# Cross attention and two expert layers on one core: the first layer's weights kept in single precision, a shorter first run of two batches, and the state rows prepared in two pieces

## The chip, the core and the metric

The kernel runs on one core of a Trainium2 chip. Five engines work side by side, each through its own instructions in order: TensorE (PE, matrix products), VectorE (DVE), ScalarE (ACT), GpSimd (POOL) and SyncE (SP), which here does nothing but start DMA transfers. An engine that needs another's result waits on a semaphore at the head of its queue, and all that stands behind the waiting instruction waits with it. The metric is device time in microseconds of one launch. The time before is the median of three runs; the profile is a fourth execution.

## The reference, cut to what matters

```python
# x: 8 batches, 8 heads, 512 tokens, 64 wide; state: 8, 8, 32, 64
a = softmax(x @ state^T / 8);   xread = a @ state          # "a" stage
a2 = softmax(state @ x^T / 8);  sread = a2 @ x             # "b" stage
z = concat(xread, sread)        # 8*512 + 8*32 = 4352 rows of 512
z = (sigmoid(z @ w_gate) * (z @ w_val)) @ w_out            # d_ff 1536
r = relu(z @ w_in); out = (r * r) @ w_out2                 # d_ff 2048
```

The expert weights arrive as float64, that is as two 32-bit words an element.

## The kernel before, in words

**Numbers.** Every product is made of three TensorE products of a value's high and low part: high by high, high by low, low by high (`mm3`, L183 to L185). A float64 weight tile of 128x512 is turned to these parts by a *conversion*: ACT extracts (L116, L118), DVE shapes and joins the bits (L119, L123, L127, L131) into a single-precision tile `c`, ACT casts its high part (L138), DVE subtracts for the low part (L139). `c` comes from a pool of two buffers.

**Layer 1 and its units.** The 1536 columns of layer 1 are 12 pieces f of 128; two pieces make one of six *chunks* (`ch`). The attention matrix `a` is not multiplied by the state first; the states are multiplied by the weights instead: for each chunk, `state_weights` multiplies four pairs of heads of four batches (m=0: batches 0 to 3, m=1: batches 4 to 7) by the chunk's converted weights; ACT copies the product from PSUM (`go`, L514, L518; with m=1 DVE makes the second copy), `store_g` writes it to memory (`gd`), and `load_g`, `split_gw` fetch it for one batch and one piece (`gi`, `gg`). A *unit* is one batch and one piece: `front_x` (six matmuls psg and a sigmoid on ACT, six matmuls psv, DVE's product, then the split into `gh` on ACT, L190, and `gl` on DVE, L191) and `back1` (twelve matmuls into `acc`). A unit is 24 matmuls of 512 columns. The converted weights, high and low, 512 KB a tile, go to memory once (`wd<-w`, 24 tiles). They are read again for m=1 (`wagain`, chunks 1 to 5) and for the state rows (`ws`).

**The order.** Units 0 to 23 are batches 0 to 3 with pieces 0 to 5 each (`HALF`), units 24 to 47 the same batches with pieces 6 to 11, units 48 to 95 batches 4 to 7 whole; 96 to 107 are the 256 state rows (`u_s` = 96), whose left operand is `sp`, the split of `xs_t`. All other work is handed out by `spread(steps, start, end)`, in units: chunk 2 from 1.2 to 3, the attention of batch 1 (`att_a[1]`) from 1 to 4, of batch 2 from 4 to 8, of batch 3 from 8 to 12, chunks 3 to 5 from 11.5 to 23.5, the m=1 chunks from 24.5 to 51.5, the state attention `att_b` from 45 + 5b. The last step of `att_b`, `b7`, copies a transposed piece to `xs_t` with four small copies, by turns on DVE (L467) and ACT (L465). A scheduler then fixes each engine's instructions in one order. Layer 2's weights are prepared in units 30 to 90 and layer 2 follows the state block.

Of the kernel before, what the change touches and what calls it, by code (L numbers as in the profile page):

```python
# [8 lines left out]
F32 = mybir.dt.float32  # L9
# [23 lines left out]
def kernel(  # L33
# [50 lines left out]
    xs_p = one.enter_context(tc.tile_pool(name="xsp", bufs=1, side="right"))  # L84
    aa_p = gen.enter_context(tc.tile_pool(name="aa", bufs=QB, side="right"))
    gi_p = gen.enter_context(tc.tile_pool(name="gi", bufs=2, side="right"))
    gg_p = gen.enter_context(tc.tile_pool(name="gg", bufs=2, side="right"))
    go_p = gen.enter_context(tc.tile_pool(name="go", bufs=3, side="right"))
    wr_p = gen2.enter_context(tc.tile_pool(name="wr", bufs=2, side="right"))
# [71 lines left out]
    def width(b):  # L161
# [6 lines left out]
    w_dram = {  # L168
        (ch, c): dram.tile([P, 2, 512], F32, name=f"wd{ch}_{c}")
        for ch in range(NCH) for c in range(NPAIR)  # L170
# [128 lines left out]
    def group_stages(b, g, both):  # L299
# [156 lines left out]
        def b7():  # L456
            w = v.pop("w")
            ps = at_p.tile([P, 2, 64], F32, tag="at", name="ps_so")
            nc.tensor.transpose(ps.rearrange("p a b -> p (a b)"), w, ident)
            for p in range(2):  # L460
                for i in range(2):
                    to = xs_t[D * p : D * (p + 1), 2 * g + i, b * NS : (b + 1) * NS]
                    src = ps[D * i : D * (i + 1), p, NS * i : NS * (i + 1)]
                    if i:
                        nc.scalar.copy(out=to, in_=src)  # L465
                    else:
                        nc.vector.tensor_copy(to, src)  # L467

# [31 lines left out]

    def conv_gv(ch, c, raw):
        gv[ch, c] = wr_p.tile([P, 2, 512], F32R, tag="w", name="w")
        convert(raw, gv[ch, c], False)

    def state_weights(ch, c, m):
        w = gv.pop((ch, c))
        if m == (ch < ONCE):
            nc.sync.dma_start(out=w_dram[ch, c], in_=w.bitcast(F32))
        ps = [at_p.tile([P, 512], F32, tag="at", name="ps_g") for j in range(2)]
        for j in range(2):  # L510
            sh, sl = (st_t[:, i, c, j, :] for i in range(2))
            mm3(ps[j], sh, sl, w[:, 0, :], w[:, 1, :], True, True)
        o = go_p.tile([P, 2, 512], F32, tag="go", name="go")
        nc.scalar.copy(out=o[:, 0, :], in_=ps[0])  # L514
        if m:
            nc.vector.tensor_copy(o[:, 1, :], ps[1])
        else:
            nc.scalar.copy(out=o[:, 1, :], in_=ps[1])  # L518
        g_out[ch, c, m] = o
# [11 lines left out]

    ONCE = 1

    def chunk_steps(ch, m, outs):
# [6 lines left out]
        def load(n):  # L541
            k, i = jobs[n]
            if ready:
                gv[ch, i] = raw_p.tile([P, 2, 512], F32R, tag="raw", name="wagain")
                nc.sync.dma_start(out=gv[ch, i].bitcast(F32), in_=w_dram[ch, i])
                return
            raws[n] = load_pair(ch, i) if k == "p" else load_raw(row_src(w_out1, i))

        def conv(n):
            k, i = jobs[n]  # L550
            if k == "p":
                conv_gv(ch, i, raws.pop(n))
            else:
                conv_out1(i, raws.pop(n))

        steps += [lambda: load(0), lambda: load(1)]
        for n in range(len(jobs) + 2):
            if n < len(jobs):
                if not ready:
                    steps.append(lambda n=n: conv(n))  # L560
                if not ready and n + 2 < len(jobs):
                    steps.append(lambda n=n: load(n + 2))
# [48 lines left out]

    def split_states():
        t = two["sp"].tile([P, 2, KD, NSTATE], F32R, name="sp")
        nc.scalar.copy(out=t[:, 0], in_=xs_t)
        nc.vector.tensor_sub(out=t[:, 1], in0=xs_t, in1=t[:, 0].bitcast(F32))
        s_parts["a"] = t

    def load_gv(ch, c):
        w = two["S"].tile([P, 2, 512], F32R, tag="w", name="ws")
        nc.sync.dma_start(out=w.bitcast(F32), in_=w_dram[ch, c])  # L620
        gv[ch, c] = w

    def front_s(b, f):
# [563 lines left out]

    HALF = NF1 // 2
    segments = [(b, 0, HALF) for b in range(QB)] + [(b, HALF, NF1) for b in range(QB)]
    segments += [(b, 0, NF1) for b in range(QB, B + 1)]  # L1190
# [38 lines left out]
    spread(chunk_steps(1, 0, outs[1]), 0, 1)  # L1229
    spread(chunk_steps(2, 0, outs[2]), 1.2, 3)  # L1230
    spread(att_a[1], 1, 4)
    spread(att_a[2], 4, 8)
    spread(att_a[3], 8, 12)
    for ch in range(3, NCH):
# [9 lines left out]
    for b in range(B):  # L1244
        start = 45 + 5 * b
        spread(att_b[b], start, start + 7)
# [5 lines left out]

    spread([close_gen], u_s - 0.6, u_s)
    spread([split_states], u_s - 0.55, u_s)
    spread([open_x_after_att], u_s - 0.5, u_s)
# [7 lines left out]
    for i, (b, f, lo, hi) in enumerate(units):  # L1263
# [7 lines left out]
        elif ff == 0:  # L1271
            for c in range(NPAIR):
                spread([lambda ch=ch, c=c: load_gv(ch, c)], max(i - 3, u_s - 0.4) + c / 50, i)
    for b in range(QB):
# [110 lines left out]
```

## Time and profile before

| what | value |
|---|---|
| runs | 1487.66, 1490.57, 1492.42 us; median 1490.57 |
| the profiled execution | 1494.57 us, span 1492.8 us |
| mean granted TensorE clock | 0.981 of full speed |
| units 0 to 23 start to end | 50.1 to 239.3 us |
| unit 5 / unit 9 / unit 24 start | 110.8 / 134.8 / 239.3 us |
| first matmul of the state block | 738.5 us |

The profiled execution lies 4.0 us above the median. A busy engine is one that runs an instruction; a wait is named by what ended it. The span's stages have different limits, so the stages are to be read one by one.

### The profile page before, as it was taken

To read this page: it belongs to the slowest core of one execution; us is meant where nothing else is said; L and a number is where in the kernel's file an instruction comes from. 1 tells how busy PE (TensorE), PEld (TensorE's weight loads), DVE (VectorE), ACT (ScalarE), POOL (GpSimd) and SP (SyncE) were. 2 spreads that over 40 slices of the span, in tenths; PEclk is the share of its full clock that TensorE was granted. 3 is DMA by queue.
4 is the path that set the end of the run, shared out by engine and by line. 5 is a ranking of instruction groups with operands and counts; after the bars stand their busy time and mean duration, and the time that the engine had idled before them with its cause. 6 is when DMAs were issued, how large, how long until landed. Compare 5 with 4: busy or idle time off the path is not lost.

```text
span 1492.8 us, 21831 instructions
## 1 busy us (share of the span) xinstructions
PE 1414.5 (95%) x7416; PEld 1204.0 (81%) x7416; DVE 1033.3 (69%) x1675; ACT 895.4 (60%) x1593; POOL 299.6 (20%) x264
## 2 busy tenths in 40 slices
PE   5769999999998889999899999899999999999998
PEld 3558878887787667888798888689999999988998
DVE  6886887568788998654534656665788479754665
ACT  6875877456668777654425855565566556564433
POOL 1112112233344454433103433200000000000000
PEclk9879999999999999999999999999999999999999
DMA  9995799699998885432586965765568555876675
GB/s 259 328 279 120 207 326 352 211 333 309 330 304 288 230 239 169 122 102 75 177 324 229 320 238 196 230 226 184 191 208 279 182 198 186 275 232 215 238 226 177
DMA packets 293375, 347.50 MB, mean 233 GB/s; under 512 B 108048, under 2 KB 204816, under 8 KB 293264
## 3 DMA queue, kind: packets, MB, share of 16 engines
q1 hardware_dynamic: 290992, 345.32, 72.1%
q8 instruction: 59, 0.97, 0.3%
q10 hardware_dynamic: 2272, 0.79, 0.2%
q14 instruction: 52, 0.43, 0.1%
HBM read 248.51 MB, written 97.52 MB: 232 GB/s over the span
## 4 chain that ended last, share of the span: by engine, by line
PE 70%; DMA 9%; DVE 9%; ACT 7%; issue 3%; POOL 1%; SPq 1%; DVEq 0%; ACTq 0%; POOLq 0%
PE o L185 7%; PE o L183 7%; PE o L184 7%; PE acc L183 4%; PE acc L184 4%; PE acc L185 4%; PE px L183 3%; PE px L184 3%; PE px L185 3%; PE psg L183 2%; PE psg L184 2%; PE psv L183 2%; PE psg L185 2%; PE psv L184 2%; PE psv L185 2%
## 5 line engine op out<-in xcount | busy, mean ns | idle before, releaser
L585 POOL TENSOR_TENSOR gg<-gi,gg 128x512 fp32r<-128x512 f32 x96 | 132.4, 1380 | 322.1 <-ACT gg L584 308.6
L183 PE MATMUL o<-wp,gh 128*128 128x256 f32 x672 | 188.8, 283 | 1.8 <-DMA wp<-wt 1.6
L184 PE MATMUL o<-wp,gh 128*128 128x256 f32 x672 | 188.7, 283 | 0.0
L185 PE MATMUL o<-wp,gl 128*128 128x256 f32 x672 | 185.4, 283 | 0.0
L184 PE MATMUL acc<-gl,o 128*128 128x512 f32 (+1 forms) x432 | 166.8, 387 | 6.4 <-DVE gl L191 6.2
L185 PE MATMUL acc<-gh,o 128*128 128x512 f32 (+1 forms) x432 | 164.9, 382 | 0.0
L183 PE MATMUL acc<-gh,o 128*128 128x512 f32 (+1 forms) x432 | 140.2, 381 | 2.1 <-ACT gh L190 2.1
L183 PEld LDWEIGHTS o<-wp,gh 128*128 128x128 f32 x672 | 128.3, 191 | 5.6 <-ACT g2s L964 1.4
L184 PEld LDWEIGHTS o<-wp,gh 128*128 128x128 f32 x672 | 128.5, 191 | 2.6
L185 PEld LDWEIGHTS o<-wp,gl 128*128 128x128 f32 x672 | 126.6, 191 | 1.2
L1090 DVE TENSOR_TENSOR y<-o,y 128x512 f32<-128x512 f32 x144 | 97.0, 685 | 35.1 <-PE o L185 34.3
L191 DVE TENSOR_TENSOR gl<-g,gh 128x512 fp32r<-128x512 f32 (+1 forms) x108 | 92.1, 853 | 28.2 <-ACT gh L190 27.6
L183 PE MATMUL px<-xh,wi 128*128 128x512 f32 x256 | 101.1, 396 | 6.0 <-DMA wi<-wi 5.0
L184 PEld LDWEIGHTS acc<-gl,o 128*128 128x128 f32 x432 | 82.5, 191 | 25.7 <-DVE gl L191 10.9
L184 PE MATMUL px<-xl,wi 128*128 128x512 f32 x256 | 100.9, 394 | 0.0
L185 PE MATMUL px<-xh,wi 128*128 128x512 f32 x256 | 100.1, 392 | 0.0
L606 DVE TENSOR_TENSOR g<-psv,sg 128x512 f32<-128x512 f32 x96 | 65.4, 682 | 46.6 <-PE psv L185 38.4
L183 PEld LDWEIGHTS acc<-gh,o 128*128 128x128 f32 x432 | 81.0, 189 | 18.2 <-ACT gh L190 2.7
L185 PEld LDWEIGHTS acc<-gh,o 128*128 128x128 f32 x432 | 82.5, 191 | 14.8
L190 ACT CAST gh<-g 128x512 fp32r<-128x512 f32 (+1 forms) x108 | 64.3, 596 | 47.0 <-DVE g L606 29.0
L599 ACT ACTIVATE sg<-psg 128x512 f32<-128x512 f32 x96 | 57.2, 596 | 55.4 <-PE psg L185 55.0
L183 PE MATMUL psg<-a,gg 128*128 128x512 f32 x192 | 77.5, 404 | 9.7 <-ACT sg L599 8.1
(215 smaller groups left out, 3793.1 us busy)
## 6 DMA issues: line engine op xcount, KB each, us to landing
wi<-wi SPq DMA_DIRECT2D x256, 256.0 KB, 3.9
gd<-go SPq DMA_DIRECT2D x192, 128.0 KB, 4.5
gi<-gd SPq DMA_DIRECT2D x96, 256.0 KB, 4.1
wp<-wt SPq DMA_DIRECT2D x96, 256.0 KB, 3.5
wp<-wo SPq DMA_DIRECT2D x72, 256.0 KB, 3.5
wi<-wa SPq DMA_DIRECT2D x32, 512.0 KB, 4.9
wo<-wo SPq DMA_DIRECT2D x32, 512.0 KB, 4.3
wd<-w SPq DMA_DIRECT2D x24, 512.0 KB, 4.9
```

The source lines that it names most:

```text
L183: nc.tensor.matmul(ps, lh, rh, start=start, stop=False, skip_group_check=more)
L184: nc.tensor.matmul(ps, lh, rl, start=False, stop=False, skip_group_check=more)
L185: nc.tensor.matmul(ps, ll, rh, start=False, stop=stop, skip_group_check=more)
L190: nc.scalar.copy(out=gh[:, :n], in_=g32[:, :n])
L191: nc.vector.tensor_sub(out=gl[:, :n], in0=g32[:, :n], in1=gh[:, :n].bitcast(F32))
L585: nc.gpsimd.tensor_sub(out=t[:, 1], in0=src, in1=t[:, 0].bitcast(F32))
L599: sig = nc.scalar.activation(out=sg, in_=ps, func=AF.Sigmoid)
L606: nc.vector.tensor_mul(out=g32, in0=ps, in1=sg)
L1090: nc.vector.tensor_add(out=y, in0=ps[to, j], in1=y)
```

## The change: what it does

The weights of layer 1 are kept in memory as the single-precision tile `c`: 256 KB instead of 512 KB. The store moves into the conversion and reads `c` itself. Who reads the tile again (`wagain`, `ws`) loads 256 KB and splits it once more, an ACT cast and a DVE subtraction (`split_again`). Units 0 to 3 are now batch 0 with pieces 0 to 3, units 4 to 7 batch 1 with pieces 0 to 3, 8 to 13 and 14 to 19 batches 2 and 3 with six pieces, 20 to 27 and 28 to 35 the remaining eight of batches 0 and 1, 36 to 47 the remaining six of 2 and 3. Chunk 2 is first needed by unit 12 instead of unit 4, the attention of batch 1 by unit 4 instead of 6, of batch 2 by 8 instead of 12, of batch 3 by 14 instead of 18. All four copies of `b7` are on ACT; the state attention starts two units sooner; `sp` is split for batches 0 to 6 first, batch 7 later.

```diff
-        (ch, c): dram.tile([P, 2, 512], F32, name=f"wd{ch}_{c}")
+        (ch, c): dram.tile([P, 512], F32, name=f"wd{ch}_{c}")
...
-                    if i:
-                        nc.scalar.copy(out=to, in_=src)
-                    else:
-                        nc.vector.tensor_copy(to, src)
+                    nc.scalar.copy(out=to, in_=src)
...
+    def conv_gv(ch, c, raw, m):
+        w = gv[ch, c] = wr_p.tile([P, 2, 512], F32R, tag="w", name="w")
+        cf = to_single(raw, False)
+        nc.scalar.copy(out=w[:, 0, :], in_=cf)
+        nc.vector.tensor_sub(out=w[:, 1, :], in0=cf, in1=w[:, 0, :].bitcast(F32))
+        if m == (ch < ONCE):
+            nc.sync.dma_start(out=w_dram[ch, c], in_=cf)
+
+    def split_again(w, sub):
+        nc.scalar.copy(out=w[:, 0, :], in_=w[:, 1, :].bitcast(F32))
+        sub(out=w[:, 1, :], in0=w[:, 1, :].bitcast(F32), in1=w[:, 0, :].bitcast(F32))
...
-        if m == (ch < ONCE):
-            nc.sync.dma_start(out=w_dram[ch, c], in_=w.bitcast(F32))
...
-                gv[ch, i] = raw_p.tile([P, 2, 512], F32R, tag="raw", name="wagain")
-                nc.sync.dma_start(out=gv[ch, i].bitcast(F32), in_=w_dram[ch, i])
+                w = gv[ch, i] = raw_p.tile([P, 2, 512], F32R, tag="raw", name="wagain")
+                nc.sync.dma_start(out=w[:, 1, :].bitcast(F32), in_=w_dram[ch, i])
...
-    HALF = NF1 // 2
-    segments = [(b, 0, HALF) for b in range(QB)] + [(b, HALF, NF1) for b in range(QB)]
+    FIRST = (4, 4, 6, 6)
+    segments = [(b, 0, FIRST[b]) for b in range(QB)] + [(b, FIRST[b], NF1) for b in range(QB)]
...
-    spread(chunk_steps(2, 0, outs[2]), 1.2, 3)
-    spread(att_a[1], 1, 4)
-    spread(att_a[2], 4, 8)
-    spread(att_a[3], 8, 12)
+    spread(chunk_steps(2, 0, outs[2]), 4, 7.5)
+    spread(att_a[1], 1, 2.6)
+    spread(att_a[2], 2.6, 5)
+    spread(att_a[3], 7, 10.5)
...
-        start = 45 + 5 * b
+        start = 43 + 5 * b
...
-    spread([close_gen], u_s - 0.6, u_s)
-    spread([split_states], u_s - 0.55, u_s)
+    spread([close_gen], u_s - 1.5, u_s)
+    spread([lambda: split_states(0, B - 1)], u_s - 1.4, u_s)
+    spread([lambda: split_states(B - 1, B)], u_s - 0.55, u_s)
...
-                spread([lambda ch=ch, c=c: load_gv(ch, c)], max(i - 3, u_s - 0.4) + c / 50, i)
+                at = max(i - 3, u_s - (0.6 if ch else 1.45))
+                spread([lambda ch=ch, c=c: load_gv(ch, c)], at + c / 50, i)
+                spread([lambda ch=ch, c=c: split_gv(ch, c)], min(at + 1, i - 0.4) + c / 50, i)
```

**TensorE around unit 4.** Before, the twelve matmuls of unit 3's `acc` are followed by batch 1's transposes (`ps_xt`) and scores (`ps_s`), and only then by unit 4, batch 0's piece 4, whose weights chunk 2 has made by then:

```order
L184 MATMUL acc_764<-gl,o_690 128x512
L185 MATMUL acc_764<-gh,o_690 128x512
L318 MATMUL ps_xt<-ident,xtok 128x128 x8
L183 MATMUL ps_s_1179<-xth,diag 128x512
L184 MATMUL ps_s_1179<-xtl,diag 128x512
L185 MATMUL ps_s_1179<-xth,diag 128x512
...
L183 MATMUL psg<-a,gg 128x512
```

In the changed kernel unit 4, now batch 1's piece 0, stands behind other scores, and chunk 2's first product `ps_g` comes only behind it:

```order
L185 MATMUL ps_s_955<-xth,diag 128x512
L183 MATMUL psg<-a,gg 128x512
L183 MATMUL psv<-a,gg 128x512
...
L185 MATMUL psv<-a,gg 128x512
L318 MATMUL ps_xt<-ident,xtok 128x128 x8
L183 MATMUL ps_s_1051<-xth,diag 128x512
...
L183 MATMUL ps_g<-w,st_t 128x512
```

Chunk 2 has moved from ahead of unit 4 to behind its start, and the second batch's attention from behind to ahead.

**ScalarE in an early conversion of layer 1's weights, ahead of unit 1.** Before, the step that fills the shared tile `c` (L118) waits for DVE alone:

```order
L116 ACTIVATE q<-raw 128x512 [waits DMAHW5_49,DMAHW2_49]
L369 CAST a<-a_417 128x512 [waits DVE_49]
L118 ACTIVATE c<-raw 128x512 [waits DVE_49]
L514 COPY go<-ps_g 128x512 [waits DMAHW6_49,DMAHW1_49,DMAHW7_49,DMAHW0_49,PE_49]
L518 COPY go<-ps_g 128x512 [waits PE_49]
L138 CAST w<-c 128x512 [waits DVE_49]
L116 ACTIVATE q<-raw 128x512 [waits DMAHW6_49,DMAHW5_49]
L118 ACTIVATE c<-raw 128x512 [waits DVE_49]
```

In the changed kernel it waits for the transfer (`DMAHW`) that reads the tile two conversions earlier; between that conversion's cast (L501) and the L118 stand eight other ACT instructions:

```order
L501 CAST w<-c 128x512 [waits DVE_49]
L337 COPY s_494<-ps_s_487 128x512 [waits DMAHW2_49,PE_49]
L116 ACTIVATE q<-raw 128x512 [waits DMAHW5_49,DMAHW2_49]
L369 CAST a<-a_417 128x512 [waits DVE_49]
L517 COPY go<-ps_g 128x512 [waits DMAHW6_49,DMAHW1_49,DMAHW7_49,DMAHW0_49,PE_49]
L521 COPY go<-ps_g 128x512 [waits PE_49]
L501 CAST w<-c 128x512 [waits DVE_49]
L116 ACTIVATE q<-raw 128x512 [waits DMAHW6_49,DMAHW5_49,Activation_49]
L351 ACTIVATE e_511<-e_511 128x512 [waits DVE_49]
L118 ACTIVATE c<-raw 128x512 [waits DMAHW3_49,Activation_49]
```

The wait for DVE has become a wait for a store.

**ScalarE ahead of the state block.** Before, the copies of the last `b7` alternate with DVE, and one cast makes `sp`:

```order
L465 COPY xs_t<-ps_so 64x32 [waits DVE_49]
L900 CAST xh<-xin 128x512
L900 CAST xh<-t 128x512
L465 COPY xs_t<-ps_so 64x32 [waits DVE_49]
L900 CAST xh<-t 128x512
L614 CAST sp<-xs_t 128x1024 [waits Activation_49]
```

In the changed kernel the cast of seven batches stands 16 rows ahead of that of the eighth, the repeated splits of the weights (`ws`) in between:

```order
L507 CAST ws<-ws 128x512 [waits DMAHW0_49]
L683 COPY y<-acc_7130 128x512 [waits PE_49]
L464 COPY xs_t<-ps_so 64x32 [waits PE_49]
L464 COPY xs_t<-ps_so 64x32 x3
L911 CAST xh<-xin 128x512
L507 CAST ws<-ws 128x512 [waits DMAHW1_49]
L507 CAST ws<-ws 128x512 [waits DMAHW2_49]
L623 CAST sp<-xs_t 128x4x32 [waits Activation_49]
```

The four copies now stand together, and the last cast is of 32 columns of each of four blocks.

## Rows read from the trace of the kernel before

**Rows 1.** The page: busy time of the engines; the chain; one kind of transfer.

```profile
PE 1414.5 (95%) x7416; PEld 1204.0 (81%) x7416; DVE 1033.3 (69%) x1675; ACT 895.4 (60%) x1593; POOL 299.6 (20%) x264
...
PE 70%; DMA 9%; DVE 9%; ACT 7%; issue 3%; POOL 1%; SPq 1%; DVEq 0%; ACTq 0%; POOLq 0%
...
wd<-w SPq DMA_DIRECT2D x24, 512.0 KB, 4.9
```

**Rows 2.** Windows by stage: us, busy of PE, PEld, DVE, ACT, POOL, clock, DMA, GB/s.

```profile
50.10:105.90 55.80, 41.66 (x168) 31.41 (x168) 47.89 (x91) 44.53 (x76) 8.01 (x8) 0.87 1.00 317
...
117.10:187.20 70.10, 70.10 (x311) 58.02 (x311) 52.43 (x87) 48.90 (x80) 15.22 (x15) 1.00 0.64 168
...
340.00:440.90 100.90, 98.11 (x432) 79.10 (x431) 81.61 (x131) 64.66 (x110) 35.62 (x33) 1.00 0.98 315
440.90:585.60 144.70, 127.80 (x560) 101.61 (x558) 130.09 (x210) 107.32 (x196) 70.95 (x57) 0.95 0.81 248
728.40:746.70 18.30, 12.81 (x59) 11.06 (x58) 10.46 (x19) 7.48 (x15) 0.00 (x0) 0.81 0.94 337
746.70:796.00 49.30, 49.30 (x405) 48.95 (x405) 15.67 (x34) 14.09 (x32) 0.00 (x0) 1.00 0.69 254
```

**Rows 3.** Groups of instructions in 50.1 to 105.9 us: busy, mean ns; idle before.

```profile
L116 ACT ACTIVATE q<-raw 128x512 uint16<-128x512 uint32 x12 | 9.3, 790 | 0.0
L131 DVE CUSTOM_DVE_ANT_0 c<-c,q 128x1024 uint16<-128x1024 uint16 x12 | 8.1, 682 | 0.1
L118 ACT ACTIVATE c<-raw 128x512 f32<-128x512 f32 x11 | 7.3, 662 | 0.9 <-DVE w L139 0.9
...
L127 DVE TENSOR_SCALAR q<-raw 128x512 uint16<-128x512 uint16 x12 | 5.4, 456 | 0.0
L139 DVE TENSOR_TENSOR w<-c,w 128x512 fp32r<-128x512 f32 x7 | 5.2, 740 | 0.8 <-ACT w L138 0.8
...
L119 DVE TENSOR_SCALAR c<-c 128x512 f32<-128x512 f32 x11 | 4.6, 417 | 1.4 <-ACT c L118 1.3
L123 DVE TENSOR_SCALAR c<-c 128x512 uint32<-128x512 uint32 x11 | 4.5, 418 | 0.1
L138 ACT CAST w<-c 128x512 fp32r<-128x512 f32 x7 | 4.4, 631 | 0.0
L325 DVE TENSOR_TENSOR xtl<-ps_xt,xth 128x512 fp32r<-128x512 f32 x6 | 4.0, 682 | 0.0
```

**Rows 4.** Timeline 84 to 106.5 us: start, length, instruction, idle before and its releaser.

```profile
94.67 1.06 PE L318 MATMUL ps_xt<-ident,xtok 128*128 128x128 f32 x8 [2.75 <-DMA xtok<-in_x_dram]
...
101.84 0.77 PE L183 MATMUL ps_s<-xth,diag 128*128 128x512 f32 x1 [6.11 <-DVE xtl L325]
...
105.93 0.79 PE L183 MATMUL psg<-a,gg 128*128 128x512 f32 x1 [1.19 <-ACT gg L584]
```

**Rows 5.** The stores of `wd` (512 KB) in 20 to 110 us: time to landing.

```profile
DMA to landing us min/median/max: 3.8/5.3/7.6
```

**Rows 6.** The stores of `sd` (256 KB) in the same stretch: time to landing.

```profile
DMA to landing us min/median/max: 2.2/3.8/6.9
```

**Rows 7.** The DVE copies of `b7`: count, min/median/max ns.

```profile
L467 DVE COPY xs_t<-ps_so x32: 144/183/185, 445.6 to 736.2; 64x32 f32<-64x32 f32 x32
```

**Rows 8.** The waits of TensorE in 440.9 to 585.6 us: total, times, longest.

```profile
PE psg L183 <- ACT sg L599: 7.0, 3, 2.9
PE acc L184 <- DVE gl L191: 5.2, 5, 2.2
```

**Rows 9.** One more subtraction of two SBUF tiles (layer 2's weights): min/median/max ns.

```profile
L748 DVE TENSOR_TENSOR wa<-c,wa x32: 649/684/1789, 289.4 to 569.1; 128x512 fp32r<-128x512 f32 x32
```

**Rows 10.** Timeline at the state block's start, 733 to 752 us.

```profile
738.50 0.58 PE L183 MATMUL psg<-sp,ws 128*128 128x256 f32 x1 [4.12 <-ACT sp L614]
739.40 1.22 DVE L615 TENSOR_TENSOR sp<-xs_t,sp 128x1024 fp32r<-128x1024 f32 x1
```

**Rows 11.** The loads of `ws` (512 KB) for the state block: time to landing.

```profile
DMA to landing us min/median/max: 3.2/6.6/9.4
```

More of the change, by code (lines that the diff above doesn't have):

```diff
@@ L85 @@
     aa_p = gen.enter_context(tc.tile_pool(name="aa", bufs=QB, side="right"))
+    go_p = gen.enter_context(tc.tile_pool(name="go", bufs=3, side="right"))
     gi_p = gen.enter_context(tc.tile_pool(name="gi", bufs=2, side="right"))
     gg_p = gen.enter_context(tc.tile_pool(name="gg", bufs=2, side="right"))
-    go_p = gen.enter_context(tc.tile_pool(name="go", bufs=3, side="right"))
     wr_p = gen2.enter_context(tc.tile_pool(name="wr", bufs=2, side="right"))
@@ L499 @@
     g_out = {}
-    def conv_gv(ch, c, raw):
-        gv[ch, c] = wr_p.tile([P, 2, 512], F32R, tag="w", name="w")
-        convert(raw, gv[ch, c], False)
+    def conv_gv(ch, c, raw, m):
[8 more added lines that the diff above has]
+        sub(out=w[:, 1, :], in0=w[:, 1, :].bitcast(F32), in1=w[:, 0, :].bitcast(F32))
     def state_weights(ch, c, m):
         w = gv.pop((ch, c))
-        if m == (ch < ONCE):
-            nc.sync.dma_start(out=w_dram[ch, c], in_=w.bitcast(F32))
         ps = [at_p.tile([P, 512], F32, tag="at", name="ps_g") for j in range(2)]
@@ L532 @@
     ONCE = 1
+    SUB2 = nc.vector.tensor_sub
     def chunk_steps(ch, m, outs):
@@ L551, in conv @@
             if k == "p":
-                conv_gv(ch, i, raws.pop(n))
+                conv_gv(ch, i, raws.pop(n), m)
             else:
@@ L558, in chunk_steps @@
             if n < len(jobs):
-                if not ready:
+                if ready:
+                    steps.append(lambda n=n: split_again(gv[ch, jobs[n][1]], SUB2))
+                else:
                     steps.append(lambda n=n: conv(n))
@@ L610, with split_states, split_gv @@
     s_parts = {}
[L612 to L616, printed above, removed]
+    def split_states(lo, hi):
+        if not s_parts:
+            s_parts["a"] = two["sp"].tile([P, 2, KD, NSTATE], F32R, name="sp")
+        cols = slice(lo * NS, hi * NS)
+        h, l = (s_parts["a"][:, i, :, cols] for i in range(2))
+        nc.scalar.copy(out=h, in_=xs_t[:, :, cols])
+        nc.vector.tensor_sub(out=l, in0=xs_t[:, :, cols], in1=h.bitcast(F32))
     def load_gv(ch, c):
         w = two["S"].tile([P, 2, 512], F32R, tag="w", name="ws")
-        nc.sync.dma_start(out=w.bitcast(F32), in_=w_dram[ch, c])
+        nc.sync.dma_start(out=w[:, 1, :].bitcast(F32), in_=w_dram[ch, c])
         gv[ch, c] = w
+    def split_gv(ch, c):
+        split_again(gv[ch, c], nc.vector.tensor_sub)
     def front_s(b, f):
```

## The prediction, made before the changed kernel ran

> **What bounds the kernel now.** The page says 95% for TensorE [rows 1], but the chain of work that ended last gives TensorE only 70%, and DMA, DVE and ACT 25% together [rows 1]: there are stages in which others set the end. The windows by stage show where. In units 0 to 3, 50.1 to 105.9 us, PE is busy 41.66 of 55.8 us, at a granted clock of 0.87, while DVE works 47.89 us (86%), ACT 44.53 (80%), and the DMA engines are busy all the time [rows 2]. From 117.1 to 187.2 us PE has no idle time. In 340 to 440.9 it lacks 2.8 us, in 440.9 to 585.6 16.9 us, with DVE at 130.09 of 144.7 (90%, the highest of any long stretch) [rows 2]. The last gap is the start of the state block, 728.4 to 746.7, where PE idles 5.5 us and the clock is 0.81 [rows 2]. So there are three places to win something, and the change touches each. The timeline of the first shows what PE waits for when unit 4 comes: an input tile from memory, DVE's `xtl`, then ACT's `gg` [rows 4]. These are small pieces of work behind much other work on busy engines and queues, and not one slow instruction.
>
> **Term 1: the first 24 units.** A conversion costs DVE 0.417 + 0.418 + 0.682 + 0.456 + 0.740 = 2.71 us and ACT 0.790 + 0.662 + 0.631 = 2.08 us [rows 3]. Chunk 2 has six. I counted the instructions ahead of unit 5's first psg in both programs. DVE has six conversions less, two subtractions of them excepted (12 x 0.417, 6 x 0.682, 6 x 0.456, 4 x 0.69: 14.6), and a few steps of a softmax less (1.8, at lengths like those of the other rows); it has two `xtl` and two copies of y more (4 x 0.68 = 2.7) [rows 3]. That is about 14 us less; ACT has some 12 us less. DVE was busy 86% of the stretch [rows 2], so unit 5 should start 14/0.88 = 16 us sooner: near 95 us instead of 110.8. The DMA gives the same: a chunk loads 3.1 MB, writes 2.1 MB of products, 1.05 MB of stores; 6 MB at 317 GB/s [rows 2] are 19 us of a full DMA.
>
> But the work isn't gone. By the same count DVE has, ahead of unit 9, as much to do as before (+1.6 us), and so has PE. Between the first psg of units 5 and 9 of the changed program stand 24.6 us of matmuls at full rate and 31 us of DVE work. If PE sets the pace unit 9 starts at 95 + 24.6 = 119.6; if DVE does, at its highest long share, 90% (440.9 to 585.6 us) [rows 2], at 95 + 34 = 129. Before, it started at 134.8. From unit 9 to 24 there are 101.3 us of matmuls where 104.5 us passed, with 87 us of DVE work. The stretch that is nearest is 50.1 to 105.9, where DVE set the pace, so I take a value near the DVE end: -8 us, bounds 0 and -18.
>
> **Term 2: units 29 to 80.** The repeated splits are 20 on ACT (0.63 each, like L138 [rows 3], 12.6 us) and 20 on DVE (0.68 each, like L748's median [rows 9], 13.7 us), in units 29 to 51.5, some 140 us. In 340 to 440.9 DVE is 19 us free and ACT 36 [rows 2], so most of it is covered by PE's work; without that cover it would cost up to 14 us. The 20 re-loads of 512 KB become 256 KB, in a stretch with the DMA at 0.98 [rows 2]: 5.2 MB less, 16 us of a full DMA. `b7` loses 32 DVE copies of 0.183 us [rows 7], 5.9 us, and the alternation with ACT; ACT gains as much. In 440.9 to 585.6 PE waits 7.0 us for ACT's sigmoid and 5.2 us for DVE's `gl` [rows 8]; the first may grow, the second shrink, and the state attention starting two units earlier moves work from the fullest stretch towards a freer one. I take -3 us, bounds -10 (most of the 12.2 us of waits gone) and +6.
>
> The Trainium skill speaks against this part: "SBUF — State Buffer", section "Who interferes with whom", has a DVE instruction with two SBUF inputs and a GpSimd instruction that reads SBUF exclude each other for their whole length. Here the longest subtraction of two SBUF tiles took 1.789 us against a median of 0.684 [rows 9], as that rule would have it, though no run here isolates it. By it the 20 subtractions could cost up to 20 x 1.1 = 22 us more of DVE. It is the third rival below.
>
> **Term 3: the state block.** Before, the last `ps_so` is followed by copies by turns, a cast and a subtraction of 1024 columns (1.04 us on ACT, 1.22 on DVE), and psg starts at 738.50 after 4.12 us of waiting; its second product waits for the subtraction [rows 10]. Now the cast of one batch's columns is left for the end (near 0.27 us), but seven or eight casts of `ws` at 0.63 and the four copies stand on ACT near it. Adding the ACT and DVE steps behind unit 95's psv up to the second product I get 11.3 us for 12.3: -1 us, bounds -3 and +3. In the state block itself PE is busy all 49.3 us, DVE 15.67, ACT 14.09 [rows 2]: 16 splits of 0.68 and 0.63 are covered. The loads halve (median landing 6.6 us [rows 11]), the split adds 1.3 us: 0, bounds 0 and +4.
>
> **Term 4: the tile that the store holds.** L118 now waits until the store of `c`, two conversions back, has landed. The 256 KB stores of `sd` took 3.8 us in the middle and 6.9 at most [rows 6], the 512 KB ones 5.3 and 7.6 [rows 5]. The eight ACT instructions between, at 0.6 to 0.8 us [rows 3], are 5.8 us in the place that the order rows show. Counted over all conversions with the work that stands between: at 5.5 us from the join to landing ACT would wait 10.6 us in sum over seven of them, at 8.0 us 41 us. At the middle the ACT waits lie in its free time (11 us in 50.1 to 105.9, 21 in 117.1 to 187.2 [rows 2]). I take 0, bounds 0 and +20.
>
> **Sum.** -8 - 3 - 1 + 0 = -12 us on the profiled execution's 1494.57 us: 1482.6. That execution lies 4.0 above the median of the runs, so against the median 1478.5 us.
>
> **Rivals.** (A) *Slower: the store holds ScalarE.* Its place is L118 in chunks 1 to 5, units 0 to 23. It decides when the stores land beyond about 6.5 us after the join; for it speak the DMA share of 1.00 and the maxima of 6.9 and 7.6 us; against it the medians. With 41 us of ACT waits, half passed on to PE through the sigmoids and casts queued behind, it is +20, less the gain of 12: +8, 1498.5 us. (B) *The gain is given back*: chunk 2 now meets the attention of batches 2 and 3 in units 4 to 11. In 117.1 to 187.2 DVE was 52.43 of 70.1 us busy; 14 us more makes 95%, above every stretch seen. Then term 1 falls to -1 and the sum to about -4: 1486.5. (C) *The second splits fill DVE*: 13.7 us and the longer subtractions, of which 19 us are free; term 2 becomes +6 and the sum -3: 1487.5. (D) *PE sets the pace all along*: -18 - 7 - 1 = -26: 1464.5.
>
> **Chances.** My forecast 0.56, D 0.12, B 0.12, C 0.07, A 0.13. What this kernel's runs can tell from no change is about 0.3%, 4.5 us. B and C lie at -3 to -4, partly over it: same 0.15; A holds cases from 0 to +20: slower 0.11; faster 0.74. The range leaves out the outer half of A and the lower part of D: 1464 to 1494.
>
> **What would show it.** In the changed profile, the start of unit 5 near 95 us (110.8), of unit 9 at 120 to 130 (134.8), of unit 24 near 231 (239.3) show term 1. If unit 9 is early and unit 24 is not, it is B. If L118's idle time has `wd` DMA as its releaser with over 15 us in sum, it is A. If the idle time of PE in 290 to 440 us grows and the subtractions of `wagain` average over 1 us, it is C. `b7` shows in the waits of 440.9 to 585.6 us (16.9 us of idle PE), the state block in the first psg (738.5) against the end of unit 95. The prediction fails if the early stretch is bound by latency of single loads and not by the work on DVE: then unit 5 moves by a few us only.

## The result, and the profile after

The changed kernel takes 1504.67 us (median of four runs, 1502.28 to 1507.23) against 1491.49 us before: a ratio of 1.0093, 95% interval 1.0064 to 1.0122. It is slower by 13 us where 12 us less was forecast, and lies outside the range.

The page of the changed kernel has TensorE as busy as before by share, and less of it in the chain than the 70% of [rows 1]:

```profile
PE 1423.6 (95%) x7416; PEld 1198.8 (80%) x7416; DVE 1057.7 (70%) x1688; ACT 925.7 (62%) x1672; POOL 301.1 (20%) x264
...
PE 62%; DMA 12%; DVE 11%; ACT 7%; issue 5%; SPq 2%; POOL 1%; DVEq 0%; ACTq 0%; POOLq 0%
```

DVE has 24 us more work and ACT 30, as the second splits and the moved copies of `b7` make it; PE's busy time grew by 9 us, and why was not looked into. What the chain lost in PE went to DMA, DVE, "issue" (time in which an engine waits for nothing that the profile shows) and SyncE's queue. The windows, cut at the starts of units 0, 5, 17, 25, 36, 53, 72 and 95, say where. The changed kernel (columns as in [rows 2]):

```profile
47.90:96.60 48.70, 42.57 (x183) 30.55 (x181) 42.30 (x71) 34.94 (x59) 11.55 (x14) 0.99 0.92 266
96.60:182.80 86.20, 78.91 (x330) 60.82 (x331) 71.02 (x123) 66.62 (x110) 16.58 (x12) 1.00 0.69 195
182.80:249.40 66.60, 60.57 (x255) 47.69 (x254) 52.52 (x89) 47.38 (x87) 14.63 (x11) 0.97 0.88 276
249.40:327.40 78.00, 75.88 (x327) 61.06 (x328) 50.41 (x71) 38.03 (x67) 21.60 (x19) 1.00 0.70 212
327.40:459.20 131.80, 122.55 (x525) 94.40 (x523) 107.30 (x174) 91.83 (x156) 43.34 (x41) 1.00 0.86 259
459.20:594.30 135.10, 125.41 (x549) 99.78 (x550) 119.21 (x191) 105.75 (x198) 70.51 (x57) 0.96 0.85 260
594.30:735.50 141.20, 141.20 (x674) 118.03 (x673) 84.26 (x126) 84.44 (x173) 52.17 (x40) 1.00 0.35 98
```

The kernel before, cut at the same units (53 to 72 is the row 440.90:585.60 of [rows 2]):

```profile
50.10:110.80 60.70, 46.53 (x181) 35.27 (x182) 51.88 (x98) 47.54 (x79) 10.98 (x10) 0.84 0.96 303
110.80:187.20 76.40, 76.40 (x343) 63.33 (x342) 57.76 (x94) 53.40 (x88) 17.81 (x17) 1.00 0.63 162
187.20:245.50 58.30, 56.13 (x246) 44.99 (x245) 50.73 (x86) 45.77 (x83) 12.88 (x12) 1.00 1.00 343
245.50:320.50 75.00, 75.00 (x331) 61.78 (x330) 41.48 (x63) 35.08 (x61) 21.45 (x19) 1.00 0.84 281
320.50:440.90 120.40, 117.61 (x518) 95.24 (x517) 98.86 (x162) 77.94 (x131) 41.56 (x39) 1.00 0.99 310
...
585.60:725.40 139.80, 139.80 (x667) 116.92 (x668) 80.92 (x139) 82.87 (x156) 51.01 (x39) 1.00 0.33 91
```

Read the second figure, the length, row against row: -12.0, +9.8, +8.3, +3.0, +11.4, -9.6, +1.4 us. The early gain is there (unit 5 starts at 96.6 us for 110.8, and the clock of that stretch is 0.99 for 0.84), and is gone by unit 25 (249.4 for 245.5). A second loss stands in units 36 to 53, most of it won back in the next stretch. The rows also show that the same units do not hold the same work: PE has 330 matmuls in units 5 to 17 for 343, and 255 for 246 in units 17 to 25. The state block is as forecast:

```profile
748.17 0.39 PE L183 MATMUL psg<-sp,ws 128*128 128x256 f32 x1 [3.71 <-ACT sp L623]
...
748.79 0.28 DVE L624 TENSOR_TENSOR sp<-xs_t,sp 128x128 fp32r<-128x128 f32 x1
749.13 0.58 PE L184 MATMUL psg<-sp,ws 128*128 128x256 f32 x1 [0.46 <-DVE sp L624]
```

Counted from unit 95's start (735.5, before 725.4) its second product comes at 13.6 us for 15.3 (740.67 by [rows 10], where the subtraction ran from 739.40 for 1.22 us).

### The profile page after: what moved, and what is told of

It reads as the page before. It is cut to its first block, busy times and chain, and to the rows that moved or that the text cites. A ratio compares the mean times of both kernels' runs of the same rounds, so it can differ in the third digit from the quotient of the medians.

```text
span 1502.2 us, 21952 instructions
## 1 busy us (share of the span) xinstructions
PE 1423.6 (95%) x7416; PEld 1198.8 (80%) x7416; DVE 1057.7 (70%) x1688; ACT 925.7 (62%) x1672; POOL 301.1 (20%) x264
## 4 chain that ended last, share of the span: by engine, by line
PE 62%; DMA 12%; DVE 11%; ACT 7%; issue 5%; SPq 2%; POOL 1%; DVEq 0%; ACTq 0%; POOLq 0%
PE o L185 7%; PE o L183 7%; PE o L184 7%; PE px L183 3%; PE acc L184 3%; PE px L184 3%; PE px L185 3%; PE acc L185 3%; PE acc L183 3%; PE psg L184 2%; PE psv L183 2%; PE psg L185 2%; PE psg L183 2%; PE psv L184 2%; PE psv L185 2%
## 5 line engine op out<-in xcount | busy, mean ns | idle before, releaser
L591 POOL TENSOR_TENSOR gg<-gi,gg 128x512 fp32r<-128x512 f32 x96 | 137.1, 1429 | 330.5 <-ACT gg L590 303.0
L183 PE MATMUL px<-xh,wi 128*128 128x512 f32 x256 | 101.3, 397 | 5.8 <-DMA wi<-wi 4.8
L183 PE MATMUL psg<-a,gg 128*128 128x512 f32 x192 | 78.4, 408 | 15.1 <-ACT sg L605 14.2
L1031 ACT ACTIVATE c<-c 128x512 f32<-128x512 f32 x72 | 45.4, 630 | 67.5 <-DVE c L991 65.1
```

What stands on the lines that cost most here:

```text
L183: nc.tensor.matmul(ps, lh, rh, start=start, stop=False, skip_group_check=more)
L591: nc.gpsimd.tensor_sub(out=t[:, 1], in0=src, in1=t[:, 0].bitcast(F32))
L1031: nc.scalar.activation(out=r, in_=c, func=AF.Relu)
```

## The experiments

Theory S: the new order gains, the single-precision storage costs. Rival O: the order gives its gain back by itself. The table holds what the traces of all kernels say; lengths in us between the starts of units, from one profiled execution each, and the ratio of the medians to the kernel before with its interval.

| kernel | start of unit 0 | 0-5 | 5-17 | 17-25 | 25-36 | 36-53 | 53-72 | ratio |
|---|---|---|---|---|---|---|---|---|
| before | 50.1 | 60.7 | 76.4 | 58.3 | 75.0 | 120.4 | 144.7 | 1 |
| before, again | 49.7 | 59.9 | 76.6 | 58.9 | 75.9 | 118.8 | 143.7 | - |
| changed | 47.9 | 48.7 | 86.2 | 66.6 | 78.0 | 131.8 | 135.1 | 1.0093 (1.0064 to 1.0122) |
| changed, again | 48.1 | 48.9 | 86.2 | 66.1 | 78.8 | 132.1 | 134.9 | - |
| order alone | 48.9 | 46.5 | 90.9 | 54.6 | 77.8 | 120.9 | 140.5 | 0.9993 (0.9975 to 1.0012) |
| order, wider | 49.5 | 47.5 | 87.2 | 58.2 | 74.9 | 121.2 | 141.1 | 0.9978 (0.9968 to 0.9989) |
| changed, two parts stored | 49.0 | 47.3 | 91.9 | 54.6 | 79.0 | 127.0 | 136.7 | 0.9990 (0.9971 to 1.0009) |
| single storage alone | 47.7 | 56.6 | 78.2 | 59.3 | 75.3 | 133.1 | 136.8 | 1.0074 (1.0052 to 1.0097) |
| ... loads made twice | 48.1 | 55.0 | 76.5 | 60.6 | 75.9 | 125.3 | 139.6 | 1.0049 (1.0032 to 1.0066) |
| ... no second splits | 48.1 | 55.9 | 76.5 | 61.9 | 78.5 | 128.4 | 139.9 | 1.0071 (1.0047 to 1.0095) |
| before + work of splits | 49.9 | 60.3 | 76.4 | 58.7 | 75.3 | 123.1 | 141.5 | 1.0022 (1.0004 to 1.0039) |
| changed, three c | 54.5 | 46.1 | 85.8 | 58.4 | 76.4 | 131.8 | 134.4 | 1.0028 (1.0012 to 1.0044) |
| ... loads made twice | 54.0 | 44.2 | 85.6 | 60.8 | 78.9 | 127.0 | 139.3 | 1.0052 (1.0034 to 1.0070) |
| ... and wider | 53.4 | 44.5 | 86.8 | 58.9 | 79.5 | 128.2 | 138.9 | 1.0042 (1.0029 to 1.0056) |
| ... three c, splits late | 53.5 | 44.9 | 85.6 | 59.4 | 77.8 | 131.4 | 145.6 | 1.0109 (1.0094 to 1.0124) |
| changed, splits late | 48.5 | 51.0 | 86.2 | 68.8 | 77.7 | 132.9 | 155.8 | 1.0169 (1.0151 to 1.0186) |
| changed, loads early | 47.9 | 50.7 | 87.7 | 65.0 | 77.2 | 130.0 | 148.2 | 1.0153 (1.0135 to 1.0171) |
| changed, splits on GpSimd | 48.1 | 48.9 | 87.8 | 64.7 | 80.4 | 137.2 | 144.7 | 1.0152 (1.0133 to 1.0172) |
| changed, no second splits | 48.1 | 49.4 | 87.8 | 64.1 | 76.2 | 130.7 | 137.3 | 1.0094 (1.0075 to 1.0113) |
| changed, old state attention | 48.1 | 48.5 | 86.2 | 65.7 | 77.3 | 129.6 | 138.1 | 1.0092 (1.0076 to 1.0107) |

**How far a stage can be trusted.** Each of the two kernels once more, with no edit.

> The kernel before once more, for one profile: how far the stages differ from one execution to the next. If units 0 to 25, 25 to 36, 36 to 53 and 53 to 72 lie within 2 us of 195.4, 75.0, 120.4 and 144.7, the differences of 8 us and more between kernels are the kernels'. If they differ by 5 us or more, single stages prove little.

> The changed kernel once more, for one profile. If the stretch of units 17 to 25 is again 64 to 69 us and that of units 36 to 53 again 129 to 134 us, both losses belong to the kernel. If either is within 3 us of the kernel before (58.3 and 120.4), it is chance.

The stages of these two pairs agree to 1.6 us at most, and both losses came again. That is the best case. Seven rows of the table (changed, changed again, splits late, loads early, splits on GpSimd, changed with no second splits, old state attention) have one and the same order on TensorE up to unit 25, and they read 48.5 to 51.0, 86.2 to 87.8 and 64.1 to 68.8 us in the first three stages. And a profiled execution need not lie near its kernel's median: order alone lies 6.3 us below, loads made twice 4.5 below, two parts stored 5.5 above, splits late 7.9 above, before + work 4.3 above, the others within 3.3 us. So a difference of less than 5 us between two single rows shows little by itself.

**The order alone, and the storage alone.** The first is the kernel before with these lines:

```diff
+    FIRST = (4, 4, 6, 6)
...
+    spread(chunk_steps(2, 0, outs[2]), 4, 7.5)
+    spread(att_a[1], 1, 2.6)
+    spread(att_a[2], 2.6, 5)
+    spread(att_a[3], 7, 10.5)
```

> The kernel before with the new order of units and its four spreads alone; storage, b7 and the state block as before. Theory S (the storage costs, the order gains): unit 5 starts near 96 us, unit 25 near 240 us (changed kernel 249.4, before 245.5), units 32 to 53 take 149 us as before, and the time is 1484 to 1488 us. Rival O (the order itself gives its gain back and more, since chunk 2 now meets the attention of batches 2 and 3): unit 25 at 247 us or later, and 1494 us or more.

Unit 5 starts at 95.4 us, unit 25 at 240.9, units 36 to 53 take 120.9: S in every stage, in the fastest of ten executions. But the medians, 1494.27 to 1493.9 us, show no gain, and that is the time that O named. Of 14.2 us less in units 0 to 5, 14.5 come back in units 5 to 17:

```profile
95.40:186.30 90.90, 85.40 (x360) 68.04 (x361) 77.51 (x134) 73.51 (x122) 19.73 (x17) 0.98 0.85 241
```

9.0 of them are busy time of PE (85.40 us for 76.40): 56 of the products `ps_g` of states and weights stand here, 16.24 us, where 27 stood before, 7.58 us; units 0 to 5 hold 6 for 30. The other 5.5 us are idle time of PE, 5.0 of it in three waits for ACT's sigmoid:

```profile
PE psg L183 <- ACT sg L599: 5.0, 3, 3.3
```

The second has the storage lines of the diff (`w_dram`, `conv_gv`, `split_again`, the loads and splits), the rest as before:

> The kernel before with the weights stored in single precision and split again, and nothing else of the change. Theory S: units 32 to 53 take 160 us or more (before 149.2), with ScalarE waiting over 10 us for the re-loaded weights, units 0 to 25 lose 0 to 6 us to the store that holds the tile c, and the time is 1498 to 1505 us. Rival O: within 4 us of the kernel before, 1488 to 1495 us.

1503.49 us, +0.74%, S again: units 36 to 53 take 133.1 us, 32 to 53 161.9, and ScalarE waits 13.2 us for the re-loaded weights. Units 0 to 25 take 194.1 for 195.4: in the old order the held tile costs nothing that shows.

**The change without the storage.** All the rest of the diff is kept:

```diff
-        (ch, c): dram.tile([P, 512], F32, name=f"wd{ch}_{c}")
+        (ch, c): dram.tile([P, 2, 512], F32, name=f"wd{ch}_{c}")
...
-                steps.append(lambda n=n: split_again(gv[ch, jobs[n][1]], SUB2))
```

> The changed kernel with the weights stored as two parts again (512 KB, no second splits, the tile c not held), with the new order, b7 on ScalarE and the state block's new timing kept. Theory S: 1480 to 1488 us, as the storage is what costs. Rival O: 1500 us or more, as the changed kernel. A third: if b7 and the state attention's earlier start cost something themselves, this kernel is slower than the one with the order alone by more than 4 us.

1492.6 us, ratio 0.999. The storage is what made the change slower; the rest together is worth nothing that can be measured. Both statements of S about the total gain (1480 to 1488) failed. One thing in this kernel's row is not the storage's: units 36 to 53 take 127.0 us, for 120.9 with the order alone, with the same 512 KB loads and, up to 367 us, the same order on all engines. What differs between the two is the state attention's earlier start, `b7`, the state block's timing and the place of one buffer pool; 53 to 72 is 3.8 us shorter in turn. These are single executions that lie far from their medians, but two later kernels with 512 KB loads and the early state attention read 127.0 and 128.2 too. So of the 11.4 us that units 36 to 53 lost, some 6 seem to come without the storage, though that costs nothing measurable in the end.

**The tile held by the store (rival A).** A third buffer, in the 2 KB a partition that are left:

```diff
+    cw_p = gen2.enter_context(tc.tile_pool(name="cw", bufs=1, side="right"))
...
+        return cv_p if turn[0] % 3 else cw_p
```

> The changed kernel with three buffers for the tile c in layer 1's conversions instead of two, so that the store no longer holds back the conversion two places on. If the held tile is what gives back the gain of units 0 to 5 (rival A of the prediction), unit 25 starts 8 us or more earlier than at 249.4 us, and the time is 1495 to 1498 us. If the hold costs little, unit 25 is within 3 us of 249.4 and the time 1502 to 1506 us.

Unit 25 starts at 244.8 us instead of 249.4, 1498.82 us in all, and the ratio falls from 1.0093 to 1.0028: between the two lines drawn (8 us, and 3 us). Units 0 to 25 take 190.3 us instead of 201.5, but that length flatters: unit 0 starts 6.6 us later, because six more products `ps_g` (48 for 42) and eight more transposes now stand ahead of it. In units 17 to 25, length 58.4 us for 66.6, with ten matmuls less:

```profile
186.40:244.80 58.40, 56.33 (x245) 44.88 (x244) 46.13 (x78) 42.60 (x78) 14.73 (x14) 1.00 0.92 279
```

By the start of unit 25 the held tile costs 4.6 us (6.6 against two parts stored, where unit 25 starts at 242.8); of the time it costs 6 us by the medians, 10 by the ratios, each to the kernel before on its own chip. ACT's idle time ahead of L118 in the changed kernel's own trace, by what ended it (us, times), shows a part of it directly:

```profile
  DMA wd<-c: 6.0, 4
  DVE wa L759: 4.2, 4
  DVE w L502: 1.7, 3
```

The stores landed in 4.0 us in the median:

```profile
DMA to landing us min/median/max: 2.1/4.0/5.8
```

So four waits, 6.0 us, though the landing is sooner than I feared. The rest comes later on: a conversion that starts late frees its input late, and the next weights are asked for late. Between the starts of units 23 and 24 of the changed kernel:

```profile
234.82 0.37 SPq L156 DMA_DIRECT2D raw<-in_moe_w_val_dram  x1
...
239.08 0.78 ACT L116 ACTIVATE q<-raw 128x512 uint16<-128x512 uint32 x1 [4.29 <-DMA raw<-in_moe_w_val_dram]
239.09 0.46 DVE L127 TENSOR_SCALAR q<-raw 128x512 uint16<-128x512 uint16 x1 [3.94 <-DMA raw<-in_moe_w_val_dram]
...
239.73 0.57 ACT L605 ACTIVATE sg<-psg 128x512 f32<-128x512 f32 x1
...
240.35 0.79 PE L183 MATMUL psg<-a,gg 128*128 128x512 f32 x1 [2.95 <-ACT sg L605]
```

The sigmoid that TensorE needs stands behind the step that waits for the load. With three buffers L118 (there L124) waits for no store in units 17 to 25 (5.3 us in three waits with two), and PE's waits there fall from 6.0 to 2.0 us; waits for loads are left. That the waits for loads follow from the held tile is argued from this. The third buffer also moves other work in the order, and what it would be worth in a kernel whose stores do not read `c` was not run.

**Where the second splits stand.** Theory Q: the cast waits for its load at the head of ScalarE's queue (14.7 us in nine waits in the changed kernel). W: it is the work, or the longer chain to the product.

```diff
             if 1 <= n <= NPAIR:
+                if ready:
+                    steps.append(lambda n=n: split_again(gv[ch, jobs[n - 1][1]], SUB2))
                 steps.append(lambda n=n: state_weights(ch, n - 1, m))
```

> The changed kernel with each second split of a re-loaded weight tile (m=1) moved one place back in the list of steps, to just ahead of the products that use it. Theory Q (the cast stands in ScalarE's queue before its load has landed, and what is behind it waits): ScalarE's waits for the re-loaded weights fall from 14.7 us to under 4, units 36 to 53 take 124 us or less (changed kernel 131.8, before 120.4), and the time is 1494 to 1499 us. Rival W (the splits' own work on busy engines, or the chain load, cast, subtraction, product): the waits of ScalarE fall, but the stretch stays at 129 us or more, and the time at 1501 us or more.

The waits halve, to 7.4 us in five:

```profile
  DMA wagain<-wd: 7.4, 5
```

The stretch stays at 132.9, and the time rises to 1520.21. Q has fallen, though its waits only halved where under 4 us were forecast. The ratio rises by 0.8%, as it does with three buffers (1.0028 to 1.0109). What was added stands mostly in units 57 to 62, where PE waits and the granted clock is 0.79. Why the later splits hurt there stays open.

```profile
494.00:552.00 58.00, 44.57 (x161) 34.39 (x160) 44.96 (x76) 43.58 (x80) 20.48 (x18) 0.79 0.82 255
```

The same units in the changed kernel:

```profile
485.40:526.20 40.80, 33.95 (x136) 25.13 (x134) 35.06 (x60) 33.16 (x62) 17.74 (x13) 0.92 0.94 265
```

The other way round, the load two steps sooner:

```diff
+                    if 1 <= n and n + 1 < len(jobs):
+                        steps.append(lambda n=n: load(n + 1))
                     steps.append(lambda n=n: split_again(gv[ch, jobs[n][1]], SUB2))
```

> The changed kernel with each re-load for m=1 (chunks 1 to 5) put ahead of the split and the products of the tiles before it, two steps sooner, so that the split finds its data. Theory K or Q (waiting for the load, in the chain or in ScalarE's queue): ScalarE's waits for these loads fall from 14.7 to under 6 us, units 36 to 53 fall from 131.8 to 126 us or less, and the time is 1494 to 1500 us. Rival W (work): 1502 to 1506 us.

12.9 us of ACT waits, 130.0 us in the stretch, 148.2 in the next, 1515.37 in all: neither theory. And both cures together, the third buffer and the late splits:

> The changed kernel with both: three buffers for the tile c, and the second splits one place back. If the held tile and the wait in ScalarE's queue are the two costs of the storage and they add up, the time is 1486 to 1492 us, not above the kernel before; if Q does not hold, it stays where three buffers alone left it, 1496 to 1501 us.

1510.88 us: the buffer's gain is there in units 17 to 25, the late splits' loss in units 53 to 72. The subtractions on another engine (`SUB2 = nc.gpsimd.tensor_sub`):

> The changed kernel with the 20 subtractions of the second splits (m=1) on GpSimd instead of VectorE. If VectorE's 13.7 us of added work is what costs, units 36 to 53 come down from 131.8 to 124 us or less and the time to 1494 to 1499 us. If the wait in ScalarE's queue (Q) costs, or the chain is longer on the slower GpSimd, the stretch stays at 129 us or more and the time at 1502 us or more.

Slower, 1516.89 us, 137.2 in the stretch. The state attention as before the change (its start and `b7`):

> The changed kernel with the state attention as before: its start at unit 45 + 5b and the four small copies by turns on VectorE and ScalarE. If the earlier start helps, by taking work out of the full stretch, units 53 to 70 get longer again and the time is 1506 us or more. If it moves the state attention into the stretch that the second splits have filled, units 36 to 53 shorten by 4 us or more and the time is 1497 to 1502 us. If neither, 1502 to 1506 us.

1508.09 us, ratio 1.0092: units 36 to 53 shorten by 2.2 us, 53 to 72 lengthen by 3.0. The line of 1506 us is passed, but the kernel before took 2.4 us more on that chip too, and the ratio is that of the changed kernel: it is worth nothing either way.

**Work, chain, or size of the load.** First the work without the chain, on the kernel before:

```diff
+    def extra_work(w):
+        nc.scalar.copy(out=spare, in_=w[:, 1, :].bitcast(F32))
+        nc.vector.tensor_sub(out=spare, in0=w[:, 1, :].bitcast(F32), in1=spare.bitcast(F32))
```

> The kernel before with 20 casts and 20 subtractions more, at the places of the second splits in the list of steps: they read a re-loaded weight tile (m=1) and write a spare tile that nobody reads. So the work and its wait for the load are there, and the products do not wait for it. Theory K (the chain load, cast, subtraction, product is what costs): units 36 to 53 within 3 us of 120.4 and the time 1491 to 1496 us. Rival W (the work on ScalarE and VectorE costs, wherever it stands): units 36 to 53 at 127 us or more (133.1 with single storage alone) and the time 1500 us or more.

123.1 us and 1494.55: 2.7 of the 11 us, and K by the lines drawn (units 53 to 72 are 3.2 us shorter in turn). Then the changed kernel, and single storage in the old order, without these splits:

```diff
-            mm3(ps[j], sh, sl, w[:, 0, :], w[:, 1, :], True, True)
+            mm3(ps[j], sh, sl, w[:, int(m and ch >= ONCE), :], w[:, 1, :], True, True)
```

> The changed kernel without the second splits for m=1 (chunks 1 to 5): the unsplit tile stands in for both parts in these products, so this kernel leaves out the split of these weights; loads, products and all else are as changed. It bounds what the splits cost, work and chain together: theories K, Q and W give units 36 to 53 near 124 us or less and 1490 to 1496 us. If the stretch stays at 129 us or more and the time at 1501 us or more, the splits are not the cause, and the state attention's earlier start or the held tile is.

> Single storage in the old order without the second splits for m=1 (chunks 1 to 5): the unsplit tile stands in for both parts in these products, so this kernel leaves out the split of these weights. Theory H: units 36 to 53 stay at 129 us or more (133.1 with the splits, 120.4 before) and the time at 1498 us or more. Rival W2: 125 us or less, and 1490 to 1496 us.

130.7 us of 131.8 in the new order, 128.4 of 133.1 in the old (just under H's 129); the ratios, 1.0094 and 1.0071, are what they were with the splits. Leaving the splits out gains nothing of the time, so K falls with Q and W. What is left to test is that the loads are half as large:

```diff
-                nc.sync.dma_start(out=w[:, 1, :].bitcast(F32), in_=w_dram[ch, i])
+                for j in range(2):
+                    nc.sync.dma_start(out=w[:, j, :].bitcast(F32), in_=w_dram[ch, i])
```

> Single storage in the old order (the kernel of the second run), with each re-load for m=1 (chunks 1 to 5) made twice, into both halves of the tile, so that 512 KB are loaded again as before; the splits stay. Theory H (halving the loads shifts the order in which the scheduler puts the work of units 36 to 53, and that order waits more on the chip): the stretch falls from 133.1 to 125 us or less. Rival W2 (the splits in the chain): it stays at 129 us or more.

125.3 us with the splits kept (the line drawn was 125): more transfers, and 7.8 us less, in an execution 4.5 us below its median. The time is 1498.79, the ratio 1.0049 for 1.0074; the two intervals overlap, so a gain in the time is likely and not shown. The row of that stretch beside those above, and the longest waits of SyncE in it:

```profile
316.10:441.40 125.30, 121.56 (x525) 95.26 (x524) 111.66 (x177) 85.67 (x146) 43.93 (x41) 1.00 0.97 300
```

```profile
SPq L348 <- ACT sg L609: 2.7, 1, 2.7
SPq L691 <- DVE yp L683: 2.6, 4, 1.5
```

With single storage alone:

```profile
317.10:450.20 133.10, 121.81 (x522) 94.68 (x521) 108.16 (x178) 86.16 (x145) 41.93 (x40) 1.00 0.89 269
```

```profile
SPq L586 <- POOL gg L594: 12.5, 5, 5.2
SPq L763 <- DVE wa L762: 7.6, 4, 2.6
SPq L532 <- DVE go L522: 5.4, 6, 2.0
```

All rows of this view for units 36 to 53 add up to 37 us before, 35 with the order alone, 41 with loads made twice, and to 60 in the changed kernel (53 in its second execution), 57 with single storage alone, 54 and 55 without the splits. Over all twenty traces the sum goes with the size of the loads: 35 to 46 us with 512 KB, 51 to 60 with 256 KB. My reading: SyncE starts every transfer in one fixed order, and with half-sized loads a scheduler that reckons with their size (`schedule_with_timeline_sim=True` in the kernel) orders the engines' work otherwise; on the chip that order makes SyncE wait for VectorE and GpSimd, and the loads behind it start late. Shown are the sums, and that the order changes: TensorE's order in single storage differs between the loads made once and twice from 245 us on. But the order also changes with the added work, and there the stretch is 2.7 us longer only; and 37 to 46 us of SyncE's waits go with 127 us and more where the state attention is early. So the size of the loads is shown to matter in this stretch; that SyncE's waits are what lengthens it, and not a sign of engines that are late for another reason, is argued.

**Both causes in the changed kernel.** The third buffer, with the loads made twice; then the wider spread as well:

> The changed kernel with three buffers for the tile c and with the re-loads for m=1 made twice (512 KB again). If the held tile and the order that the halved loads bring are its two costs, and they add up, units 17 to 25 take 60 us or less, units 36 to 53 take 127 us or less, SyncE's waits in the latter are near 40 us, and the time is 1491 to 1496 us. If the second does not carry over to the new order, 36 to 53 stay at 130 us or more and the time at 1497 to 1500 us, as with three buffers alone.

> The same, and with chunk 2 spread over units 4 to 9 and the attention of batch 3 over 8 to 12.5. If the wider spread is worth here what it was with the order alone (3 to 4 us), 1488 to 1493 us; if it is worth nothing beside three buffers, the time of the run before it.

The stages came nearly as said, 60.8 and 127.0 us, SyncE's waits 39 us. But units 53 to 72 took 139.3 for 134.4, and the time is 1502.24, outside both ranges: nothing is gained over three buffers alone. The two stretches together take 266.3 us for 266.2; that they share one stock of work, and what doesn't get done in one is done in the next, is argued from that. The spread made 1.3 us, which the intervals do not tell from nothing.

**The spread of chunk 2 (rival B), and the fastest version.** On the order alone:

```diff
-    spread(chunk_steps(2, 0, outs[2]), 4, 7.5)
+    spread(chunk_steps(2, 0, outs[2]), 4, 9)
...
-    spread(att_a[3], 7, 10.5)
+    spread(att_a[3], 8, 12.5)
```

> The kernel with the order alone, but chunk 2 spread over units 4 to 9 instead of 4 to 7.5 and the attention of batch 3 over 8 to 12.5 instead of 7 to 10.5. If the order gives its gain back because chunk 2 and the attention of batch 3 crowd the same units (rival B), units 5 to 17 take 84 us or less (90.9 with the order alone, 76.4 before) and the time is 1484 to 1490 us. If the work comes back wherever it is put, the time stays at 1490 to 1495 us.

1489.64 us, ratio 0.9978: the one kernel here whose interval lies below the kernel before, by 0.2%; against the order alone (0.9975 to 1.0012) the intervals overlap. Units 5 to 17 take 87.2 us, not 84, and the 3.7 us won there are gone in units 17 to 25 (58.2 for 54.6). Crowding is not shown to be why the gain is given back.

## Why the prediction was wrong

- **Term 1, to unit 5: right.** Unit 5 was to start near 95 and started at 96.6 us. DVE's work ahead of it fell from 89.00 to 78.22 us (74.79 with the order alone) where I had counted 14 us less, and its busy share in units 0 to 5 is 87%, 85% before.
- **Term 1, units 5 to 24: mis-sized.** Unit 9 came at 127.2 us, inside the forecast's 120 to 130. From unit 9 to 24 I reckoned with 101.3 us of matmuls where 104.5 us had passed, as if PE set the pace; it took 108.8 us with the order alone and 113.1 in the changed kernel. I took -8 us by unit 24, a start near 231; it starts at 233.9 with the order alone and at 240.3 in the changed kernel (239.3 before). Rival B, to which I gave 0.12, is what the order alone looks like in units 5 to 17, but not by its reason: DVE is busy 77.51 of 90.9 us, not 95%, and yet PE waits, for ACT's sigmoid. The error was to hold one engine's busy share for the limit. (B's sum is about -5 by its own terms, not -4, and the -7 that D takes for term 2 has no source.)
- **Term 4, taken as 0: the step that failed first.** Unit 25 starts at 249.4 us with the tile held, 242.8 with two parts stored, 244.8 with three buffers: 5 to 7 us, rival A in kind at a quarter to a third of its price of +20, and 6 to 10 of the 13 us of the time. I priced ACT's waits at L118 by landing times alone, and let them fall into its free time. The landings were short (4.0 us), and the sign I had set for A, over 15 us of such waits, did not come: 6.0 us. The rest of the cost is put down to what stands behind the waiting instruction and to the loads that start later; that part is argued.
- **Term 2, -3 us: wrong in sign.** Units 25 to 72 take 344.9 us for 340.1, +4.8, with +11.4 in units 36 to 53. Two steps failed. The earlier state attention was to be a gain by moving work out of the fullest stretch; work did move (120.9 and 140.5 us with the order alone, 127.0 and 136.7 with two parts stored), and nothing was gained by it. And "5.2 MB less" was taken as a gain with no price: the DMA's share in units 36 to 53 fell from 0.99 to 0.86, and the stretch is 5 to 8 us longer with 256 KB loads than with 512 KB (131.8 for 127.0 with three buffers; 133.1 for 125.3 in the old order). Why smaller loads lengthen it stays open. The 20 splits as work, which I had covered, are covered: 2.7 us in their stretch, nothing over units 25 to 72.
- **Rival C and the Trainium skill's rule.** "SBUF — State Buffer", section "Who interferes with whom", lets a DVE instruction with two SBUF inputs and a GpSimd instruction that reads SBUF exclude each other. The longest of the changed kernel's subtractions took 1.785 us, the median 0.692:

```profile
L508 DVE TENSOR_TENSOR wagain<-wagain x20: 644/692/1785, 245.7 to 454.0; 128x512 fp32r<-128x512 f32 x20
```

  The trace agrees with the rule: five of the twenty ran beside a GpSimd instruction and took 0.90 to 1.79 us, the fifteen others 0.69 us at most. The price is 4.2 us of DVE in all, where 22 were feared, and the mean of 0.89 us stays under C's sign of 1 us. The loss is not there: without these subtractions the changed kernel is as slow.
- **Term 3: right,** -1.7 us for -1 at the second product.

The sum was -12; the parts as measured, from unit 0's start on, are +6.1 to unit 25, +4.8 to unit 72, +1.4 to unit 95 and -0.7 behind, less 2.2 before unit 0: +9.4 us between the two profiled spans.

## What to carry to other kernels

A transfer that reads a working tile instead of the finished one puts its landing into the chain of whoever fills that tile next; count what stands behind that wait in the engine's queue, not the wait. Where a scheduler fixes the order from its own reckoning of transfers, halving a transfer is a change to all orders: compare the waits of the queue that starts the transfers before and after, and test with the old size kept. A gain in one stage is only worth what is left at the end of the next stages, so follow the starts of a few fixed units to the end, and count the work between two of them before you compare lengths: a stage can be shorter because its work has moved ahead of it.

## What the runs showed that was not expected

More bytes were faster in one stretch: 512 KB loaded instead of 256 took units 36 to 53 from 133.1 to 125.3 us with the splits kept. Two pairs of executions of one kernel agree to 1.6 us in each stage, but seven executions with one order differ by up to 4.7 us in a stage, and the totals of one kernel range over as much as 13 us (1488.84 to 1501.47 in thirty runs of the kernel before). And a shift of 20 splits by one step raised the ratio from 1.0093 to 1.0169, some 11 us, and most of it fell in units 57 to 62, behind the last of these splits, where the granted clock was 0.79.
